# Grouped 1x1 convolution: all pixels in full 128-row chunks on the two hardware DMA queues, with a hardware loop on TensorE

## The chip, the cores and the metric

The kernel runs on one core of one Trainium2 chip. The metric is the device time of one execution in microseconds (us), and lower is better. The kernel before took 528.25 us (median of 3 runs, 526.8 to 528.28). "The span" is the part of the time that the profile covers, from the first to the last instruction.

One look means one profiled run, next to runs of the kernel before on the same chip.

## The reference, cut to what matters

```python
# x: (1, 512, 512, 192) bf16;  w: (1, 1, 4, 48, 48) bf16   (kernel size 1, 4 groups of 48 channels)
xg  = x.reshape(1, 512, 512, 4, 48)
out = einsum('bhwgc,gcd->bhwgd', xg, w[0, 0])      # for each pixel and each group: 48 -> 48
return out.reshape(1, 512, 512, 192)
```

There are 262,144 pixels of 384 bytes. About 100.7 MB are read and 100.7 MB are written, and very little is computed for each byte. In the page of the kernel before, the DMA engines are busy for 90% or more of nearly every slice.

## The kernel before

A chunk is a load of some rows by 32 pixels for each row. A row is one partition of SBUF and 12,288 contiguous bytes of DRAM, and in the trace it is one DMA packet of 12,288 bytes. Normal chunks ("nat") have 128 rows. SyncE issues their loads and ScalarE their stores, both on hardware DMA queues.

Beside them run 24 "relief" chunks of 60 or 44 rows. GpSimd loads and stores them on its software DMA queue. A dummy transfer of one or five rows comes before each. The kernel's helper for it is called `move_cursor`, and I call it the cursor move. The trace shows that in 22 of the 24 relief loads one of the 16 increments lands 11.2 to 16.2 us before the second. I read that as one engine which gets no row of the relief chunk.

```python
NBI = 5; NBO = 5; NRI = 2; NRO = 2; NOB = 5; NXP = 3; NXS = 3; LOOK = 2
RELIEF = {"relA": (36, 60, 1), "relB": (52, 44, 5)}   # first partition, rows, dummy rows
N_RELIEF = 24                                          # 18 relA, 6 relB
...
        @block.gpsimd
            def load(n):
                wait_in_free(wq, n)
                i = ordinal[n] % NRI
                p0_, rows, skip = RELIEF[kinds[n]]
                move_cursor(skip)                      # the dummy transfer
                gp.dma_start(xr_sb[i][p0_:p0_ + rows, 0:sizes[n] * C], rows_view(xf, n)).then_inc(rl_sem[i], 16)
...
        @block.sync
            for n in nat_ids:
                wait_in_free(wq, n)
                b = ordinal[n] % NBI
                sp.dma_start(x_sb[b][:, 0:sizes[n] * C], rows_view(xf, n)).then_inc(ld_sem[b], 16)
...
        @block.tensor                                  # 620 groups, all unrolled
            for g in range(NG):
                if g + LOOK < NG:
                    transposes(g + LOOK)               # 6 transposes of x into PSUM
                matmuls(g)                             # 6 matmuls with block-diagonal weights
```

A group is four pixel columns: 6 transposes, a copy of the transposed pixels from PSUM to SBUF by VectorE, 6 matmuls, and the copy of the outputs by ScalarE and VectorE. A relief chunk costs as many groups as a normal one but has under half of its pixels. That is why there are 620 groups and not 512.

## Time and profile before

| | before |
|---|---|
| time, median of 4 runs beside the kernel after | 527.52 us (525.32 to 528.28) |
| span of the profiled run | 523.9 us |
| TensorE busy | 89% |
| DMA engines busy, middle of the span | 90% or more in nearly every slice |
| bytes moved by DMA | 202.4 MB, mean 386 GB/s |

These lines are from the page of the kernel before: the span, the busy time of the engines, the GB/s in 40 equal slices, the DMA queues (packets, MB, share of the time of 16 engines), the shares of the chain of waits that ended last, and one line of the DMA issues (count, KB each, median us from issue to landing).

```profile
span 523.9 us, 16823 instructions
PE 468.8 (89%) x7450; PEld 462.0 (88%) x7450; DVE 401.5 (77%) x810; ACT 413.8 (79%) x622; POOL 55.3 (11%) x106
...
GB/s 302 295 416 402 392 413 391 397 407 406 386 396 401 417 386 378 415 385 383 419 400 378 419 388 397 415 387 398 417 393 391 414 395 389 415 419 400 376 332 143
...
q1 hardware_dynamic: 8848, 84.17, 41.4%
q10 hardware_dynamic: 8640, 84.15, 39.4%
q0 software_dynamic: 5184, 33.04, 16.1%
q8 instruction: 58, 0.95, 0.7%
...
PE 53%; DMA 45%; POOL 1%; ACT 0%; issue 0%; POOLq 0%; ACTq 0%
...
xr_sb<-in_x_dram POOLq DMA_DIRECT2D x18, 720.0 KB, 19.9
```

The row of GB/s swings between about 378 and 419, although the DMA engines are busy all the time. So the swings are not idle time: some packets take longer. The window view says so directly. Its columns are the stretch in us and its length, then the busy us (and instructions) of five engines, the granted TensorE clock, the DMA share and the GB/s.

```profile
core 0: us, PE busy (x) PEld busy (x) DVE busy (x) ACT busy (x) POOL busy (x), PEclk, DMA share, GB/s
213.00:219.00 6.00, 5.41 (x87) 5.42 (x88) 4.66 (x10) 3.73 (x6) 0.00 (x0) 1.00 1.01 421
222.00:228.00 6.00, 6.00 (x104) 5.99 (x102) 5.33 (x12) 5.33 (x10) 0.23 (x1) 1.00 1.00 341
240.00:246.00 6.00, 6.00 (x109) 5.99 (x106) 5.34 (x13) 5.45 (x10) 0.00 (x0) 1.00 1.00 352
247.00:252.00 5.00, 5.00 (x84) 5.00 (x82) 4.50 (x10) 4.55 (x8) 2.03 (x4) 1.00 1.00 423
```

The DMA share is 1.00 in all four, but the second and third stretch move about a fifth less. These two are relief loads. The first is a relief store, and the fourth has no relief transfer. In the packet records of the whole trace, 24 stretches of this kind last 132 us together. A packet of 12,288 bytes takes 570 ns on average in them and 469 ns outside, and the median of all is 460.0 ns. (The prediction's 23 stretches and 125 us are an earlier count of the same records. The counts depend on where the line is drawn. Counted again, in slices of 2 us whose packets average over 510 ns, there are 25 stretches, 126 us together. This recount is given below where it differs much.)

### The profile page before, as it was taken

What the parts mean: (1) busy time and instruction counts of PE and PEld (TensorE: products, weight loads), DVE (VectorE), ACT (ScalarE), POOL (GpSimd) and SP (SyncE); (2) the same over time, 40 slices, a digit from 0 to 9 for tenths busy, and PEclk for the clock granted to TensorE, in tenths of its full rate; (3) what the DMA queues carried; (4) which work ended last, traced back from release to release, by engine and by line L of the source; (5) the groups of instructions that cost most, each with busy time, mean ns of one, the idle gap of its engine ahead of it and who ended that gap; (6) DMA issues with size and microseconds to landing.
All of it is one profiled execution on the core that took longest, in us unless ns stands there. A gap on an engine that the chain in (4) does not pass through costs nothing.

```text
span 523.9 us, 16823 instructions
## 1 busy us (share of the span) xinstructions
PE 468.8 (89%) x7450; PEld 462.0 (88%) x7450; DVE 401.5 (77%) x810; ACT 413.8 (79%) x622; POOL 55.3 (11%) x106
## 2 busy tenths in 40 slices
PE   6399999999999979879989889879979889997873
PEld 5399999999999979879979889879979879997872
DVE  5188889888888868768878778767878777886751
ACT  6199998989999968768879779778969778895752
POOL 6011011101110110010110110110110110000000
PEclk9699999999999999999999999998999998998987
DMA  8999999999999999999999999999999999999983
GB/s 302 295 416 402 392 413 391 397 407 406 386 396 401 417 386 378 415 385 383 419 400 378 419 388 397 415 387 398 417 393 391 414 395 389 415 419 400 376 332 143
DMA packets 22744, 202.43 MB, mean 386 GB/s; under 512 B 4624, under 2 KB 5648, under 8 KB 6928
## 3 DMA queue, kind: packets, MB, share of 16 engines
q1 hardware_dynamic: 8848, 84.17, 41.4%
q10 hardware_dynamic: 8640, 84.15, 39.4%
q0 software_dynamic: 5184, 33.04, 16.1%
q8 instruction: 58, 0.95, 0.7%
q14 instruction: 14, 0.11, 0.1%
HBM read 100.68 MB, written 100.66 MB: 384 GB/s over the span
## 4 chain that ended last, share of the span: by engine, by line
PE 53%; DMA 45%; POOL 1%; ACT 0%; issue 0%; POOLq 0%; ACTq 0%
DMA x_sb<-in_x_dram 42%; PE o_ps L322 30%; PE xT_ps L300 23%; DMA xr_sb<-in_x_dram 2%; POOL xr_sb L246 1%; ACT o_sb L390 0%; POOL scratch L228 0%; POOL esel L216 0%; POOL esel L212 0%; POOL ident L220 0%; POOL ident L213 0%; POOL scratch L214 0%; ACTq L57 0%; POOLq L415 0%; POOLq L216 0%
## 5 line engine op out<-in xcount | busy, mean ns | idle before, releaser
L354 DVE COPY xT_sb<-xT_ps 128x768 bf16<-128x768 bf16 (+1 forms) x620 | 322.5, 524 | 112.9 <-PE xT_ps L300 109.5
L322 PE MATMUL o_ps<-wt,xT_sb 128*128 128x144 bf16 (+1 forms) x3720 | 367.0, 236 | 0.0
L390 ACT CAST o_sb<-o_ps 128x768 bf16<-128x768 f32 x300 | 231.0, 799 | 76.1 <-PE o_ps L322 74.4
L322 PEld LDWEIGHTS o_ps<-wt,xT_sb 128*128 128x128 bf16 x3720 | 266.2, 99 | 1.4
L300 PE MATMUL xT_ps<-ident,x_sb 128*128 128x128 bf16 x2568 | 219.1, 223 | 39.9 <-DMA x_sb<-in_x_dram 39.7
L300 PEld LDWEIGHTS xT_ps<-ident,x_sb 128*128 128x128 bf16 x2568 | 168.1, 100 | 44.7 <-DMA x_sb<-in_x_dram 43.9
L390 ACT CAST or_sb<-o_ps 128x768 bf16<-128x768 f32 x134 | 101.6, 804 | 10.2 <-PE o_ps L322 7.1
L300 PE MATMUL xT_ps<-ident,xr_sb 96*128 96x96 bf16 x1152 | 81.7, 207 | 8.8 <-DMA xr_sb<-in_x_dram 8.8
L386 ACT CAST o_sb<-o_ps 128x384 bf16<-128x384 f32 x128 | 61.5, 480 | 20.0 <-PE o_ps L322 19.4
L300 PEld LDWEIGHTS xT_ps<-ident,xr_sb 96*128 96x128 bf16 x1152 | 64.6, 98 | 9.0 <-DMA xr_sb<-in_x_dram 9.0
L362 DVE CAST o_sb<-o_ps 128x384 bf16<-128x384 f32 x128 | 70.8, 553 | 1.9 <-PE o_ps L322 1.7
L228 POOL DMA_DIRECT2D scratch<-scratch x48 | 24.2, 504 | 409.3 <-DVE xT_sb L354 409.0
L362 DVE CAST or_sb<-o_ps 128x384 bf16<-128x384 f32 x58 | 32.2, 555 | 0.7
L386 ACT CAST or_sb<-o_ps 128x384 bf16<-128x384 f32 x58 | 28.7, 495 | 0.0
L243 POOL DMA_DIRECT2D out_dram<-or_sb x24 | 12.7, 527 | 0.3 <-issue 0.3
L236 POOL DMA_DIRECT2D xr_sb<-in_x_dram x24 | 12.5, 522 | 0.0
L246 POOL MEMSET xr_sb<- 128x6144 bf16 x1 | 5.2, 5207 | 0.0
L282 PE MATMUL o_ps<-w_sb,esel 48*128 48x48 bf16 x10 | 0.6, 209 | 2.6 <-DMA w_sb<-in_w_dram 2.6
L369 ACT ACTIVATE xr_sb<-xr_sb 128x3072 uint32<-128x3072 uint32 x1 | 2.8, 2763 | 0.0
L282 PEld LDWEIGHTS o_ps<-w_sb,esel 48*128 48x128 bf16 x10 | 0.4, 111 | 2.6 <-POOL esel L216 2.6
L369 ACT ACT_TABLE_LOAD x1 | 1.3, 1283 | 0.8 <-PEq L415 0.8
L339 DVE MEMSET xT_sb<- 128x384 uint32 x3 | 1.1, 378 | 1.0 <-PEq L415 1.0
(10 smaller groups left out, 2.4 us busy)
## 6 DMA issues: line engine op xcount, KB each, us to landing
x_sb<-in_x_dram SPq DMA_DIRECT2D x51, 1536.0 KB, 40.0
out_dram<-o_sb ACTq DMA_DIRECT2D x51, 1536.0 KB, 38.3
xr_sb<-in_x_dram POOLq DMA_DIRECT2D x18, 720.0 KB, 19.9
out_dram<-or_sb POOLq DMA_DIRECT2D x18, 720.0 KB, 12.3
xr_sb<-in_x_dram POOLq DMA_DIRECT2D x6, 528.0 KB, 18.8
out_dram<-or_sb POOLq DMA_DIRECT2D x6, 528.0 KB, 10.9
x_sb<-in_x_dram SPq DMA_DIRECT2D x3, 768.0 KB, 30.0
out_dram<-o_sb ACTq DMA_DIRECT2D x3, 768.0 KB, 11.9
```

The lines of the kernel that those rows point to most:

```text
L228: gp.dma_start(scratch[0:skip, 2 * nd + 1:2 * nd + 2], scratch[0:skip, 0:1]).then_inc(dm_sem, 16)
L236: gp.dma_start(xr_sb[i][p0_:p0_ + rows, 0:sizes[n] * C], rows_view(xf, n)).then_inc(rl_sem[i], 16)
L243: gp.dma_start(rows_view(of, n), or_sb[i][p0_:p0_ + rows, 0:sizes[n] * C]).then_inc(rs_sem[i], 16)
L246: gp.memset(xr_sb[i][:], 0.0).then_inc(z_sem, 1)
L300: last = pe.transpose(xT_ps[:, g % NXP, j * 128:j * 128 + rows], xb[0:rows, col:col + 128], ident[0:rows, 0:rows])
L322: last = pe.matmul(o_ps[:, v % NOB, c0:c1], lhsT=xs[:, j * 128:(j + 1) * 128], rhs=wt[:, WOFF[tc]:WOFF[tc] + (c1 - c0)], start=(tc == 0), ...
L339: dve.memset(xT_sb[i][:], 0.0).then_inc(zt_sem, 1)
L354: dve.tensor_copy(dst, src).then_inc(dve_done, 1)
L362: dve.tensor_copy(obuf(n)[:, u * UC:(u + 1) * UC], o_ps[:, v % NOB, 0:UC]).then_inc(dve_done, 1)
L369: act.memzero(xr_sb[i][:]).then_inc(z_sem, 1)
L386: ins = act.copy(ob[:, u * UC:(u + 1) * UC], o_ps[:, v % NOB, 0:UC])
L390: ins = act.copy(dst, o_ps[:, v % NOB:v % NOB + 2, 0:UC])
```

## The change

The relief chunks and the software queue go. All pixels are in 70 chunks of 128 rows on the two hardware queues, with one more input and output buffer each. TensorE's program, which is all unrolled before, becomes a hardware loop of 10 trips over a body of 48 groups. For this its waits had to stop depending on the group's number: each ring semaphore is waited for at a constant and then counted down by TensorE itself. The intent, as I read it: fewer groups, no software queue, and less fetch of TensorE's program (58 packets on the instruction queue in the page before).

```diff
-NBI = 5
-NBO = 5
-NRI = 2
-NRO = 2
-NOB = 5
-NXP = 3
-NXS = 3
-LOOK = 2
-RELIEF = {"relA": (36, 60, 1), "relB": (52, 44, 5)}
...
-N_RELIEF = 24
...
-ST_DELAY = 1
+NBI = 6
+NBO = 6
+NXP = 4
+NOB = 4
+LOOK = 3
+ST_DELAY = 2
+RING = 6
...
+    body = NBI * PPC // 4
+    loop_g0 = chunk_g0[first_full]
+    reps = max(0, (n_full * PPC // 4 - LOOK) // body)
+    loop_g1 = loop_g0 + reps * body
...
         @block.gpsimd
...
-                gp.dma_start(xr_sb[i][p0_:p0_ + rows, 0:sizes[n] * C], rows_view(xf, n)).then_inc(rl_sem[i], 16)
...
         @block.tensor
...
             def transposes(g):
...
                 if lg == 0:
-                    wait_loaded(wq, n)
+                    pe.wait_ge(ld_sem[n % NBI], 16)
...
+                if lg == 0:
+                    ins[1].then_inc(ld_sem[n % NBI], -16)
...
             def matmuls(g):
...
+                waited = [e1_sem[g % RING]]
+                if g >= 2:
+                    waited.append(fa_sem[(g - 2) % RING])
+                    if shared(g - 2):
+                        waited.append(d2_sem[(g - 2) // 3 % 2])
+                for s in waited:
+                    pe.wait_ge(s, 1)
...
+                for i, s in enumerate(waited):
+                    ins[1 + i].then_inc(s, -1)
...
-            for g in range(NG):
-                if g + LOOK < NG:
-                    transposes(g + LOOK)
-                matmuls(g)
+            for g in range(loop_g0 if reps else 0):
+                step(g)
+            if reps:
+                with pe.Fori(0, reps, 1):
+                    for g in range(loop_g0, loop_g0 + body):
+                        step(g)
+            for g in range(loop_g1 if reps else 0, NG):
+                step(g)
```

More of the change, by code (lines that the diff above doesn't have):

```diff
@@ L27 @@
 TAIL = (16, 8, 4, 4)
-NBI = 5
-NBO = 5
-NRI = 2
-NRO = 2
-NOB = 5
-NXP = 3
-NXS = 3
-LOOK = 2
-RELIEF = {"relA": (36, 60, 1), "relB": (52, 44, 5)}
-REND = 96
-RPPC = 32
-B_EVERY = 4
-N_RELIEF = 24
-FIRST_RELIEF = 4
-RELIEF_GAP = 2
-SHARE = (2, 4, 7)
-ST_DELAY = 1
+NBI = 6
[5 more added lines that the diff above has]
+RING = 6
 class Waiter:
@@ L57, in wait @@
         self.eng.wait_ge(sem, val)
-def relief_kinds(n_relief):
-    return ["relB" if B_EVERY and i % B_EVERY == B_EVERY - 1 else "relA" for i in range(n_relief)]
 def plan_chunks(npix):
     assert npix % 512 == 0, "the pixel count must be a multiple of 512"
-    for n_relief in range(N_RELIEF, -1, -1):
-        rk = relief_kinds(n_relief)
-        rest = npix - sum(RELIEF[k][1] * RPPC for k in rk)
-        if rest < 0 or rest % 512 != 0:
-            continue
-        cols = rest // 128
-        head, tail = list(HEAD), list(TAIL)
-        if cols < sum(head) + sum(tail) + PPC:
-            if n_relief:
-                continue
-            head, tail = [], []
-        mid = cols - sum(head) - sum(tail)
-        nat = head
-        while mid > 0:
-            nat.append(min(PPC, mid))
-            mid -= nat[-1]
-        nat += tail
-        chunks = [("nat", s) for s in nat]
-        pos = FIRST_RELIEF
-        for k in rk:
-            pos = min(pos, len(chunks) - len(tail))
-            chunks.insert(pos, (k, RPPC))
-            pos += RELIEF_GAP + 1
-        return chunks
-    raise AssertionError("no chunk plan")
+    cols = npix // 128
+    head, tail = list(HEAD), list(TAIL)
+    if cols < sum(head) + sum(tail) + PPC:
+        head, tail = [], []
+    mid = cols - sum(head) - sum(tail)
+    first = len(head)
+    full = mid // PPC
+    sizes = head + [PPC] * full
+    if mid % PPC:
+        sizes.append(mid % PPC)
+    return sizes + tail, first, full
 def bass_standalone__grouped__vision_kernel(nc, x, w, out):
@@ L96, in bass_standalone__grouped__vision_kernel @@
     npix = B * H * W_
-    chunks = plan_chunks(npix)
-    n_chunks = len(chunks)
-    kinds = [c[0] for c in chunks]
-    sizes = [c[1] for c in chunks]
-    nrows = [128 if k == "nat" else RELIEF[k][1] for k in kinds]
-    nat_ids = [n for n in range(n_chunks) if kinds[n] == "nat"]
-    rel_ids = [n for n in range(n_chunks) if kinds[n] != "nat"]
-    n_rel = len(rel_ids)
-    ordinal = {n: i for ids in (nat_ids, rel_ids) for i, n in enumerate(ids)}
+    sizes, first_full, n_full = plan_chunks(npix)
+    n_chunks = len(sizes)
     xf = x.rearrange("b h w c -> (b h w) c")
@@ L110, in bass_standalone__grouped__vision_kernel @@
     wv = w.rearrange("a b g c d -> c (a b g) d")
-    chunk_pix0, p0 = [], 0
-    for n in range(n_chunks):
-        chunk_pix0.append(p0)
-        p0 += nrows[n] * sizes[n]
-    assert p0 == npix
-    groups, chunk_g0 = [], []
+    col0, groups, chunk_g0, chunk_g1, c0 = [], [], [], [], 0
     for n, s in enumerate(sizes):
+        col0.append(c0)
+        c0 += s
         chunk_g0.append(len(groups))
         groups += [(n, lg) for lg in range(s // 4)]
+        chunk_g1.append(len(groups))
     NG = len(groups)
-    chunk_g1 = [chunk_g0[n] + sizes[n] // 4 for n in range(n_chunks)]
+    body = NBI * PPC // 4
+    assert body % 12 == 0
+    loop_g0 = chunk_g0[first_full]
+    reps = max(0, (n_full * PPC // 4 - LOOK) // body)
+    loop_g1 = loop_g0 + reps * body
     def shared(g):
-        return (g % 5 == 2) or ((g % 10) in SHARE)
+        return g % 3 == 1 and g < NG - 3
     dve_prog = [("wcopy", 0)]
@@ L133, in bass_standalone__grouped__vision_kernel @@
             dve_prog.append(("ev2", h))
-    dve_cnt = {op: i + 1 for i, op in enumerate(dve_prog)}
-    act_cnt = {g: g + 1 for g in range(NG)}
     def rows_view(ap, n):
-        rows, s = nrows[n], sizes[n]
-        return ap[chunk_pix0[n]:chunk_pix0[n] + rows * s, :].rearrange("(p i) c -> p (i c)", p=rows)
+        s = sizes[n]
+        return ap[128 * col0[n]:128 * (col0[n] + s), :].rearrange("(p i) c -> p (i c)", p=128)
     with ExitStack() as es:
@@ L144, in bass_standalone__grouped__vision_kernel @@
         o_sb = [es.enter_context(nc.sbuf_tensor(f"o_sb{i}", [128, PPC * C], BF16)) for i in range(NBO)]
-        xr_sb = [es.enter_context(nc.sbuf_tensor(f"xr_sb{i}", [128, RPPC * C], BF16)) for i in range(NRI)]
-        or_sb = [es.enter_context(nc.sbuf_tensor(f"or_sb{i}", [128, RPPC * C], BF16)) for i in range(NRO)]
-        xT_sb = [es.enter_context(nc.sbuf_tensor(f"xT_sb{i}", [128, 2 * UC], BF16)) for i in range(NXS)]
+        xT_sb = [es.enter_context(nc.sbuf_tensor(f"xT_sb{i}", [128, 2 * UC], BF16)) for i in range(NXP)]
         ident = es.enter_context(nc.sbuf_tensor("ident", [128, 128], BF16))
@@ L151, in bass_standalone__grouped__vision_kernel @@
         wt = es.enter_context(nc.sbuf_tensor("wt", [128, WCOLS], BF16))
-        scratch = es.enter_context(nc.sbuf_tensor("scratch", [16, 4 * max(n_rel, 1) + 8], BF16))
         xT_ps = es.enter_context(nc.psum_tensor("xT_ps", [128, NXP, 1024], BF16))
@@ L160, in bass_standalone__grouped__vision_kernel @@
         st_sem = [sem(f"st{i}") for i in range(NBO)]
-        rl_sem = [sem(f"rl{i}") for i in range(NRI)]
-        rs_sem = [sem(f"rs{i}") for i in range(NRO)]
-        z_sem = sem("z_sem")
-        zt_sem = sem("zt_sem")
-        w_sem, id_sem, e_sem, wb_sem = sem("w_sem"), sem("id_sem"), sem("e_sem"), sem("wb_sem")
-        p0_sem, p1_sem, sc_sem, dm_sem = sem("p0_sem"), sem("p1_sem"), sem("sc_sem"), sem("dm_sem")
-        t_done = sem("t_done")
-        mm_done = sem("mm_done")
-        dve_done = sem("dve_done")
@@ L170, in bass_standalone__grouped__vision_kernel @@
-        act_done = sem("act_done")
-        def xbuf(n):
-            return x_sb[ordinal[n] % NBI] if kinds[n] == "nat" else xr_sb[ordinal[n] % NRI]
-        def used_rows(n):
-            return 128 if kinds[n] == "nat" else REND
-        def obuf(n):
-            return o_sb[ordinal[n] % NBO] if kinds[n] == "nat" else or_sb[ordinal[n] % NRO]
-        def wait_loaded(wq, n):
-            k = ordinal[n]
-            if kinds[n] == "nat":
-                wq.wait(ld_sem[k % NBI], 16 * (k // NBI + 1))
-            else:
-                wq.wait(rl_sem[k % NRI], 16 * (k // NRI + 1))
@@ L188, in wait_in_free @@
-        def wait_in_free(wq, n):
-            k = ordinal[n]
-            if kinds[n] == "nat":
-                if k >= NBI:
-                    wq.wait(t_done, chunk_g1[nat_ids[k - NBI]])
-            elif k >= NRI:
-                wq.wait(t_done, chunk_g1[rel_ids[k - NRI]])
-        def wait_out_free(wq, n):
-            k = ordinal[n]
-            if kinds[n] == "nat":
-                wq.wait(st_sem[k % NBO], 16 * (k // NBO))
-            else:
-                wq.wait(rs_sem[k % NRO], 16 * (k // NRO))
@@ L203, in wait_evacuated @@
-        def wait_evacuated(wq, n):
-            wq.wait(act_done, act_cnt[chunk_g1[n] - 1])
-            dv = [dve_cnt[("ev2", g)] for g in range(chunk_g0[n], chunk_g1[n]) if shared(g)]
-            if dv:
-                wq.wait(dve_done, max(dv))
+        w_sem, id_sem, e_sem, wb_sem, wc_sem = (sem(s) for s in ("w_sem", "id_sem", "e_sem", "wb_sem", "wc_sem"))
+        p0_sem, p1_sem = sem("p0_sem"), sem("p1_sem")
+        t_done, mm_done = sem("t_done"), sem("mm_done")
+        e1_sem = [sem(f"e1_{i}") for i in range(RING)]
@@ L209, in _ @@
+        fa_sem = [sem(f"fa_{i}") for i in range(RING)]
+        d2_sem = [sem(f"d2_{i}") for i in range(2)]
+        def wait_out_free(wq, n):
+            wq.wait(st_sem[n % NBO], 16 * (n // NBO))
         @block.gpsimd
         def _(gp):
-            wq = Waiter(gp)
             gp.memset(esel[:], 1.0).then_inc(p0_sem, 1)
             gp.memset(ident[:], 1.0).then_inc(p1_sem, 1)
-            gp.memset(scratch[:], 0.0).then_inc(sc_sem, 1)
             gp.wait_ge(p0_sem, 1)
@@ L222, in _ @@
                              channel_multiplier=1).then_inc(id_sem, 1)
-            gp.wait_ge(sc_sem, 1)
-            state = {"nd": 0}
-            def move_cursor(skip):
-                nd = state["nd"]
-                gp.dma_start(scratch[0:skip, 2 * nd + 1:2 * nd + 2], scratch[0:skip, 0:1]).then_inc(dm_sem, 16)
-                state["nd"] = nd + 1
-            def load(n):
-                wait_in_free(wq, n)
-                i = ordinal[n] % NRI
-                p0_, rows, skip = RELIEF[kinds[n]]
-                move_cursor(skip)
-                gp.dma_start(xr_sb[i][p0_:p0_ + rows, 0:sizes[n] * C], rows_view(xf, n)).then_inc(rl_sem[i], 16)
-            def store(n):
-                wait_evacuated(wq, n)
-                i = ordinal[n] % NRO
-                p0_, rows, skip = RELIEF[kinds[n]]
-                move_cursor(skip)
-                gp.dma_start(rows_view(of, n), or_sb[i][p0_:p0_ + rows, 0:sizes[n] * C]).then_inc(rs_sem[i], 16)
-            for i in range(1, NRI if n_rel else 0, 2):
-                gp.memset(xr_sb[i][:], 0.0).then_inc(z_sem, 1)
-            if n_rel:
-                gp.wait_ge(z_sem, NRI)
-            for n in rel_ids[:NRI]:
-                load(n)
-            for k, n in enumerate(rel_ids):
-                store(n)
-                if k + NRI < n_rel:
-                    load(rel_ids[k + NRI])
-            for i in range(NRO):
-                cnt = len(rel_ids[i::NRO])
-                if cnt:
-                    gp.wait_ge(rs_sem[i], 16 * cnt)
-            if state["nd"]:
-                gp.wait_ge(dm_sem, 16 * state["nd"])
         @block.sync
@@ L265, in _ @@
             sp.dma_start(w_sb[:], wv).then_inc(w_sem, 16)
-            for n in nat_ids:
-                wait_in_free(wq, n)
-                b = ordinal[n] % NBI
+            for n in range(n_chunks):
+                if n >= NBI:
+                    wq.wait(t_done, chunk_g1[n - NBI])
+                b = n % NBI
                 sp.dma_start(x_sb[b][:, 0:sizes[n] * C], rows_view(xf, n)).then_inc(ld_sem[b], 16)
@@ L272, in _ @@
         def _(pe):
-            wq = Waiter(pe)
             def build_weights():
-                wq.wait(e_sem, 1)
-                wq.wait(w_sem, 16)
+                pe.wait_ge(e_sem, 1)
+                pe.wait_ge(w_sem, 16)
                 last = None
-                for (tc, r, g, c0) in WBLOCKS:
+                for (tc, r, g, c0_) in WBLOCKS:
                     s0 = ESHIFT - r
-                    col = WOFF[tc] + c0
+                    col = WOFF[tc] + c0_
                     last = pe.matmul(o_ps[:, NOB - 1, col:col + CG], lhsT=esel[:, s0:s0 + 128],
@@ L288, in transposes @@
                 if g == 0:
-                    wq.wait(id_sem, 1)
+                    pe.wait_ge(id_sem, 1)
                 if lg == 0:
-                    wait_loaded(wq, n)
-                xb = xbuf(n)
-                rows = used_rows(n)
-                last = None
+                    pe.wait_ge(ld_sem[n % NBI], 16)
+                xb = x_sb[n % NBI]
+                ins = []
                 for ul in range(2):
@@ L299, in transposes @@
                         j = ul * 3 + tc
-                        last = pe.transpose(xT_ps[:, g % NXP, j * 128:j * 128 + rows],
-                                            xb[0:rows, col:col + 128], ident[0:rows, 0:rows])
-                last.then_inc(t_done, 1)
-            def matmuls(g):
-                xs = xT_sb[g % NXS]
-                last = None
+                        ins.append(pe.transpose(xT_ps[:, g % NXP, j * 128:(j + 1) * 128],
+                                                xb[:, col:col + 128], ident[:]))
@@ new lines, in transposes @@
+                if lg == 0:
+                    ins[1].then_inc(ld_sem[n % NBI], -16)
+                ins[-1].then_inc(t_done, 1)
+            def matmuls(g):
+                xs = xT_sb[g % NXP]
+                waited = [e1_sem[g % RING]]
+                if g == 0:
+                    pe.wait_ge(wc_sem, 1)
+                if g >= 2:
[4 more added lines that the diff above has]
+                    pe.wait_ge(s, 1)
+                ins = []
@@ L307, in matmuls @@
                 for ul in range(2):
                     v = 2 * g + ul
-                    if ul == 0:
-                        need = dve_cnt[("ev1", g)]
-                        if g >= 3:
-                            if shared(g - 3):
-                                need = max(need, dve_cnt[("ev2", g - 3)])
-                            else:
-                                wq.wait(act_done, act_cnt[g - 3])
-                        wq.wait(dve_done, need)
-                    elif g >= 2:
-                        wq.wait(act_done, act_cnt[g - 2])
@@ L319, in matmuls @@
                     for tc in range(3):
                         j = ul * 3 + tc
-                        c0, c1 = COLR[tc]
-                        last = pe.matmul(o_ps[:, v % NOB, c0:c1], lhsT=xs[:, j * 128:(j + 1) * 128],
-                                         rhs=wt[:, WOFF[tc]:WOFF[tc] + (c1 - c0)],
-                                         start=(tc == 0), stop=(tc == 2), skip_group_check=True)
-                last.then_inc(mm_done, 1)
+                        c0_, c1_ = COLR[tc]
+                        ins.append(pe.matmul(o_ps[:, v % NOB, c0_:c1_], lhsT=xs[:, j * 128:(j + 1) * 128],
+                                             rhs=wt[:, WOFF[tc]:WOFF[tc] + (c1_ - c0_)],
+                                             start=(tc == 0), stop=(tc == 2), skip_group_check=True))
@@ L327, in _, with step @@
+                for i, s in enumerate(waited):
+                    ins[1 + i].then_inc(s, -1)
+                ins[-1].then_inc(mm_done, 1)
+            def step(g):
+                if g + LOOK < NG:
+                    transposes(g + LOOK)
+                matmuls(g)
             build_weights()
@@ L337, in _ @@
             wq = Waiter(dve)
-            for i in range(NXS if n_rel else 0):
-                dve.memset(xT_sb[i][:], 0.0).then_inc(zt_sem, 1)
-            if n_rel:
-                dve.wait_ge(zt_sem, NXS)
-            waited_chunk = -1
             for (op, g) in dve_prog:
@@ L345, in _ @@
                     wq.wait(wb_sem, 1)
-                    dve.tensor_copy(wt[:], o_ps[:, NOB - 1, 0:WCOLS]).then_inc(dve_done, 1)
+                    dve.tensor_copy(wt[:], o_ps[:, NOB - 1, 0:WCOLS]).then_inc(wc_sem, 1)
                     continue
@@ L350, in _ @@
                     wq.wait(t_done, g + 1)
-                    rows = used_rows(n)
-                    src = xT_ps[:, g % NXP, 0:2 * UC].rearrange("p (j c) -> p j c", c=128)[:, :, 0:rows]
-                    dst = xT_sb[g % NXS][:].rearrange("p (j c) -> p j c", c=128)[:, :, 0:rows]
-                    dve.tensor_copy(dst, src).then_inc(dve_done, 1)
-                else:
-                    if waited_chunk != n:
-                        waited_chunk = n
-                        wait_out_free(wq, n)
+                    dve.tensor_copy(xT_sb[g % NXP][:], xT_ps[:, g % NXP, 0:2 * UC]).then_inc(e1_sem[g % RING], 1)
+                else:
+                    wait_out_free(wq, n)
                     wq.wait(mm_done, g + 1)
@@ L361, in _ @@
                     v = 2 * g + 1
-                    dve.tensor_copy(obuf(n)[:, u * UC:(u + 1) * UC],
-                                    o_ps[:, v % NOB, 0:UC]).then_inc(dve_done, 1)
+                    dve.tensor_copy(o_sb[n % NBO][:, u * UC:(u + 1) * UC],
+                                    o_ps[:, v % NOB, 0:UC]).then_inc(d2_sem[g // 3 % 2], 1)
         @block.scalar
@@ L367, in _ @@
             wq = Waiter(act)
-            for i in range(0, NRI if n_rel else 0, 2):
-                act.memzero(xr_sb[i][:]).then_inc(z_sem, 1)
             pending = []
             def store(n):
-                wait_evacuated(wq, n)
-                b = ordinal[n] % NBO
+                b = n % NBO
                 act.dma_start(rows_view(of, n), o_sb[b][:, 0:sizes[n] * C]).then_inc(st_sem[b], 16)
@@ L381, in _ @@
                 wq.wait(mm_done, g + 1)
+                while pending and pending[0][1] <= g:
+                    store(pending.pop(0)[0])
                 v = 2 * g
-                ob = obuf(n)
+                ob = o_sb[n % NBO]
                 if shared(g):
@@ L387, in _ @@
                 else:
-                    assert v % NOB != NOB - 1
                     dst = ob[:, lg * 2 * UC:(lg + 1) * 2 * UC].rearrange("p (u c) -> p u c", u=2)
                     ins = act.copy(dst, o_ps[:, v % NOB:v % NOB + 2, 0:UC])
-                ins.then_inc(act_done, 1)
-                if g == chunk_g1[n] - 1 and kinds[n] == "nat":
+                ins.then_inc(fa_sem[g % RING], 1)
+                if g == chunk_g1[n] - 1:
                     pending.append((n, g + ST_DELAY))
-                while pending and pending[0][1] <= g:
-                    store(pending.pop(0)[0])
             for (n, _) in pending:
+                act.wait_ge(fa_sem[(chunk_g1[n] - 1) % RING], 1)
                 store(n)
             for b in range(NBO):
-                cnt = len(nat_ids[b::NBO])
+                cnt = len(range(b, n_chunks, NBO))
                 if cnt:
-                    act.wait_ge(st_sem[b], 16 * cnt)
+                    wq.wait(st_sem[b], 16 * cnt)
 _INS = ['x', 'w']
```

## The prediction

> **What bounds the kernel now.** DMA: the page's slices show the 16 DMA engines 90% busy or more from slice 2 to 38, moving 201.3 MB at 384 GB/s; the chain of waits gives 45% to loads, 53% to TensorE. TensorE (89% busy) is close: relief chunks fill only 60 or 44 of 128 rows, so 620 groups of 0.75 us (timeline) are 465 us; 512 full groups are 384.
>
> In the packet records a 12,288-byte packet takes 460 ns at best, 491 ns on average, and nearly all the excess sits in 23 stretches of 3 to 14 us, together about 125 us, where it averages 574 ns (469 ns outside). These coincide with the relief *loads* on the software queue, not with its stores. The windows view agrees: 222-228 us 341 GB/s, 240-246 us 352; 247-252 us 423, and 213-219 us (a relief store) 421. Outside them the mean is about 417 GB/s.
>
> Bytes by engine, worked out from the relief shapes (60 rows = 15 engines, 44 rows = 11): the engine always left out carries 10.5 MB, most others 12.88 MB: 1,048 packets x 491 ns = 515 us, plus about 10 us of start and end gives the span. One of 16 increments of most transfers lands 15 to 25 us before the next. The relief exists, I infer, because TensorE's instruction fetch (queue table: 58 packets of 16 KB, 0.95 MB, 1.07 us each, 62 us) falls on that engine.
>
> **What the change does.** Removed: the software queue (33 MB) and with it, I expect, the slow stretches; 108 groups of TensorE, VectorE and ScalarE work. Every engine gets 12.58 MB = 1,024 packets: at about 465 ns 476 us; by the observed 417 GB/s, 483 us. Moved: the skipped engine gets 2.1 MB more (about 78 us), affordable only if the loop ends most instruction fetch. [...] If it stays resident, I expect about 10 fetch packets, 11 us, not 58. Added: up to three waits per group and ten trips of the loop; TensorE's slack (384 of 480 us) should hide them.
>
> **Sum.** 476 to 483 us of DMA + 11 us fetch on one engine + 2 us start + 5 us end = 494 us span, +4 us between span and measured time = 498 us. The DMA saving is on the critical path; the freed compute is not.
>
> **If the loop refetches its body each trip**, one engine carries 12.58 MB plus about 50 us of fetch: about 540 us. I give that 20 to 25%, hence 488 to 538. Chances: faster 0.75, same 0.12, slower 0.13.
>
> **What would show it right:** no slow stretches, mean 12 KB packet under 470 ns; 405-420 GB/s over the middle of the span; instruction queue 58 packets to 15 or fewer; TensorE waiting for loads; the 16 landings of a load within a few us. **Wrong:** instruction packets near 50 and one engine landing far behind the rest (fetch not removed); packets still at 490 ns (relief loads not the cause); TensorE idle once per 48 groups (branching); or groups over 0.94 us with loads landed (waits, four output banks).

What is cut here is the argument about the size of the loop's body, which no trace or run showed. No term of the sum is cut: it came to 494 us of span and 498 us of time. Its 11 us of fetch are 10 packets at the 1.07 us that a fetch packet took in the trace before. The 10 was my estimate. (58 packets for 620 groups are 7.5 for the 80 groups that TensorE's program now holds: the 48 of the body and the 32 outside the loop.) That all fetch falls on one engine was an inference. The bytes by engine, with 15 engines for 60 rows and 11 for 44, are an estimate from the shapes of the chunks. Later traces show four rows for each of 16 engines in loads of 64 rows and 15 engines for 60 rows; for 44 rows nothing shows it.

## The result, and the profile after

The kernel after takes 494.0 us (median of 4 runs, 493.32 to 495.58), against 527.52 us before. The ratio is 0.9379, with a 95% interval from 0.935 to 0.9409, so the change is faster. A ratio here is the mean time of one kernel's runs over that of the other's of the same rounds, so it is not quite the ratio of the medians that are quoted.

The lines of the page after that answer to those of before:

```profile
span 492.4 us, 14343 instructions
PE 415.0 (84%) x6154; PEld 389.1 (79%) x6154; DVE 358.1 (73%) x683; ACT 345.6 (70%) x513; POOL 1.3 (0%) x8
...
GB/s 294 414 418 425 427 427 429 430 429 429 430 429 429 429 428 427 427 429 427 428 430 429 429 430 430 429 430 427 428 427 429 428 429 429 429 429 427 279 253 143
...
q1 hardware_dynamic: 10288, 100.69, 48.5%
q10 hardware_dynamic: 10080, 100.67, 48.3%
q8 instruction: 7, 0.11, 0.1%
...
DMA 71%; PE 24%; ACT 3%; issue 1%; ACTq 1%; SPq 0%
```

Two of the same stretches in the window view after, with the columns as before:

```profile
222.00:228.00 6.00, 4.80 (x75) 4.49 (x73) 4.33 (x10) 4.08 (x7) 0.00 (x0) 1.00 1.02 432
240.00:246.00 6.00, 4.84 (x75) 4.50 (x72) 4.17 (x8) 4.33 (x8) 0.00 (x0) 1.00 1.01 430
```

The largest wait of TensorE in the view of waits (who waited for what: us in total, times, longest us):

```profile
PE xT_ps L184 <- DMA x_sb<-in_x_dram: 58.3, 54, 3.2
```

The last load in the chain of waits (start, duration, what), with the transposes that it releases:

```profile
453.46 28.42 DMA x_sb<-in_x_dram
481.93 0.82 PE xT_ps L184 x6
```

The bytes are the same (HBM read and written together differ by less than 0.1%), and the DMA engines are as busy as before. They move them faster: 425 to 430 GB/s through the middle, against a swing from 378 to 419. The mean packet of 12,288 bytes went from 492.5 to 462.3 ns. TensorE now waits for loads 54 times. The chain of waits moved from 53% TensorE to 71% DMA. The queue of instruction fetch went from 58 packets to 7.

So far everything looks as predicted, the total included (498 predicted, 494 measured). The experiments ask whether the reasons were right.

### The profile page after: what moved, and what is told of

Read it like the earlier page. It is cut to its first block, busy times and chain, and to the rows that moved or that the text cites. A ratio compares the mean times of both kernels' runs of the same rounds, so it can differ in the third digit from the quotient of the medians.

```text
span 492.4 us, 14343 instructions
## 1 busy us (share of the span) xinstructions
PE 415.0 (84%) x6154; PEld 389.1 (79%) x6154; DVE 358.1 (73%) x683; ACT 345.6 (70%) x513; POOL 1.3 (0%) x8
## 4 chain that ended last, share of the span: by engine, by line
DMA 71%; PE 24%; ACT 3%; issue 1%; ACTq 1%; SPq 0%
DMA x_sb<-in_x_dram 71%; PE o_ps L207 13%; PE xT_ps L184 10%; ACT o_sb L274 3%; ACTq L258 1%; SPq L155 0%; SPq L150 0%; ACTq L47 0%
## 5 line engine op out<-in xcount | busy, mean ns | idle before, releaser
L242 DVE COPY xT_sb<-xT_ps 128x768 bf16<-128x768 bf16 x512 | 283.8, 555 | 114.8 <-PE xT_ps L184 109.7
L274 ACT CAST o_sb<-o_ps 128x768 bf16<-128x768 f32 x342 | 267.0, 799 | 107.9 <-PE o_ps L207 101.6
L184 PE MATMUL xT_ps<-ident,x_sb 128*128 128x128 bf16 x3072 | 257.2, 220 | 58.3 <-DMA x_sb<-in_x_dram 58.3
L207 PE MATMUL o_ps<-wt,xT_sb 128*128 128x144 bf16 (+1 forms) x3072 | 297.4, 233 | 10.4 <-ACT o_sb L274 10.1
L184 PEld LDWEIGHTS xT_ps<-ident,x_sb 128*128 128x128 bf16 x3072 | 195.0, 98 | 70.0 <-DMA x_sb<-in_x_dram 68.9
L207 PEld LDWEIGHTS o_ps<-wt,xT_sb 128*128 128x128 bf16 x3072 | 211.5, 98 | 24.5 <-issue 17.7
L271 ACT CAST o_sb<-o_ps 128x384 bf16<-128x384 f32 x170 | 81.6, 480 | 33.3 <-PE o_ps L207 24.0
L248 DVE CAST o_sb<-o_ps 128x384 bf16<-128x384 f32 x170 | 94.2, 554 | 8.1 <-PE o_ps L207 7.0
```

The source lines that it names most:

```text
L184: ins.append(pe.transpose(xT_ps[:, g % NXP, j * 128:(j + 1) * 128], xb[:, col:col + 128], ident[:]))
L207: ins.append(pe.matmul(o_ps[:, v % NOB, c0_:c1_], lhsT=xs[:, j * 128:(j + 1) * 128], rhs=wt[:, WOFF[tc]:WOFF[tc] + (c1_ - c0_)], start=(tc ...
L242: dve.tensor_copy(xT_sb[g % NXP][:], xT_ps[:, g % NXP, 0:2 * UC]).then_inc(e1_sem[g % RING], 1)
L248: dve.tensor_copy(o_sb[n % NBO][:, u * UC:(u + 1) * UC], o_ps[:, v % NOB, 0:UC]).then_inc(d2_sem[g // 3 % 2], 1)
L271: ins = act.copy(ob[:, u * UC:(u + 1) * UC], o_ps[:, v % NOB, 0:UC])
L274: ins = act.copy(dst, o_ps[:, v % NOB:v % NOB + 2, 0:UC])
```

## The experiments

The expectations use letters, and a letter stands for what the text says beside it. In short: A is my theory as it then stood. In the first batch it is the prediction's: that TensorE's instruction fetch falls on the engine which the relief left out, so that the relief can only go if the loop comes. In the second batch it is that the software queue's loads stretch the packets, and, for the run on the slow engine, that taking work from that engine shortens the time. B is the first rival: the fetch does not matter, and the relief costs more than it gives, with or without the loop. C and D are the rivals in the second batch: C puts the stretch on the shape and placement of the relief loads, whichever queue issues them, and D says that software loads of full rows are harmless. E is the rival for the run on the slow engine: the engine is the wrong one, or software stores stretch packets as well. F is C made exact: the place of a partial load decides, so that 64 rows stretch the packets from partition 36 and not from partition 32.

The texts say "engine 4" for the engine that had 11 labels in the second experiment. The number is only a name: no trace gives an engine's number.

"Slow stretches" are counted in the packet records as in the section on the profile before. All kernels below gave the correct result.

### Take the relief out, and nothing else

```diff
-N_RELIEF = 24
+N_RELIEF = 0
```

This is the kernel before, still unrolled, with its own buffers and waits.

> The kernel before with the relief chunks taken out (all chunks 128 rows, two hardware queues, TensorE still unrolled). Theory A (fetch falls on one engine, slow stretches come from the relief loads): mean 12 KB packet falls from 491 to under 470 ns, no slow stretches, about 48 fetch packets (58 x 512/620) of 1.07 us all on one engine, which ends about 51 us or more after the others would; time 535 to 555 us, slower than before (528). Rival B (the fetch does no harm, the software queue was pure loss): time 494 to 502 us, no engine far behind. Rival C (the slow stretches are not due to relief loads): mean packet stays near 490 ns, time about 550 us or more.

Measured: 493.99 us (4 runs, 492.95 to 494.04), ratio 0.9351 (0.9322 to 0.9379). Theory A failed, and B held. From the page of this run:

```profile
span 492.1 us, 13861 instructions
...
GB/s 283 422 426 426 425 427 427 425 427 426 428 428 427 429 426 426 428 426 425 425 427 429 428 426 428 428 427 428 424 426 425 426 428 427 429 428 425 362 305 137
...
q8 instruction: 48, 0.79, 0.6%
```

There are 48 fetch packets, and yet the row of GB/s is as flat as after the whole change. There is no slow stretch, and the mean packet takes 463.0 ns. One edited number gives all of the gain that the large diff gives.

### Tell the engines apart, in the kernel after

The trace does not name the engine of a DMA packet. This run adds 15 tiny loads, of 1 to 15 rows, on the load queue, after chunk 30:

```diff
                 sp.dma_start(x_sb[b][:, 0:sizes[n] * C], rows_view(xf, n)).then_inc(ld_sem[b], 16)
+                if n == 30:
+                    for r in range(1, 16):
+                        m = 1 if r == 1 else 32 * r
+                        sp.dma_start(lab[0:r, 512 * r:512 * r + m], rows_view(xf, 30)[0:r, 0:m]).then_inc(lab_sem, 16)
+            sp.wait_ge(lab_sem, 16 * 15)
```

> The kernel after, plus 15 tiny loads (r rows, r = 1 to 15, each of its own size) issued once on the load queue, so that in the packet records every DMA engine can be named by how many of them it served [...]. Time: within 1% of the kernel after (494 us). Theory A (some engine is slow for a reason of its own): the lagging chain of packets, 478 ns per 12 KB packet against 460 ns on the others, is one named engine, and it is not one that fetched instructions during the loop. Rival B (the lag is leftover instruction fetch): the lagging chain is the one that has the 16 KB or 8 KB instruction packets.

Measured: 494.18 us (one run), so the labels cost nothing that this run shows. I chained the packets into 16 back-to-back sequences, which I take for the 16 engines, and the sequences had 0, 1, 2, ... 15 labels, each count once. So an engine can be told by its number of labels.

The sequence that lagged had 11 labels. I call it the slow engine. Its packets of 12,288 bytes took 478.4 ns on average, while 13 engines without other traffic took 460.0 ns. In the stretch looked at (150 to 320 us) the slow engine had no fetch packet at all, and TensorE's own fetch packets (16,384 bytes) all lay before 53 us or after 468 us. So it is slow for some other reason.

### Unroll TensorE again, in the kernel after

```diff
-    reps = max(0, (n_full * PPC // 4 - LOOK) // body)
+    reps = 0
```

The labels are in this run and the next too.

> The kernel after with TensorE's loop taken out (same instructions, unrolled), and the same 15 tiny label loads. Theory A: about 48 to 52 fetch packets instead of 7, all on one named engine, whose transfers end late; the other 15 engines wait for it; time 535 to 555 us, within 1.5% of the kernel before without relief. Rival B (the loop matters little, all of the gain is the removal of relief): 494 to 502 us.

Measured: 497.39 us (4 runs, 496.19 to 498.28), ratio 0.9414 (0.9385 to 0.9443). Theory A failed, and B held. The instruction queue in the page of this run:

```profile
q8 instruction: 50, 0.82, 0.6%
```

The fetch is back, but it is spread over eight of the 16 sequences (about 6 packets each). A fetch packet takes 966 ns on average, so each of the eight gives about 6 us to it (50 packets of 0.966 us over eight). The trace shows a little more: behind 48 of the 50 the next data packet took 887 ns on average and not 460, so each engine gives nearer 9 us (an estimate). The slow engine, the one with 11 labels, has none. It is still the slowest, with 480.4 ns per packet. Beside it the other engines have some 18 us to spare (an estimate: 1,024 packets, 478 ns against 460), so fetch on them can cost little.

The loop is worth 3.4 us here (494.0 against 497.4, from two batches, and the two sets of runs do not overlap), which is 0.7%. It only wins back what the new structure costs: the old unrolled structure without relief ran at 493.99 us on the same chip as this run. Which part of the new structure costs it is open.

### A loop body of twice the length

```diff
-    body = NBI * PPC // 4
+    body = 2 * NBI * PPC // 4
```

That is 96 groups and 5 trips.

> The kernel after with a loop body of 96 groups in 5 trips instead of 48 in 10 [...], and the label loads. Theory A (what counts is that the body stays resident): the fetch comes back, about 45 to 55 packets, time 530 to 555 us as unrolled. Rival B (a loop as such saves the fetch, or the whole body is held at this size too): 7 to 15 packets and 494 us.

Measured: 497.64 us (4 runs, 497.37 to 498.15), ratio 0.943 (0.9402 to 0.9457). The instruction queue, from the page, and one line of the view of waits:

```profile
q8 instruction: 56, 0.92, 0.7%
...
PE xT_ps L191 <- issue: 24.2, 5, 6.3
```

The body of 48 groups runs ten times with 7 fetch packets in the whole kernel. The body of 96 has 56, more than the 50 of the unrolled program, which I read as a body that is fetched anew on its trips. It also stalls TensorE four times, once for each jump back between the five trips, by 5.6 to 6.3 us (the fifth wait in that line is one of 0.2 us, at 73.7 us). So the part of theory A about the fetch held, and its consequence for the time did not: refetching everything costs 3.6 us against the kernel after, and not the 40 us and more of my second case. TensorE has slack for the stalls: its waits for loads fell from 58.3 to 30.8 us. The engines that carry the fetch have it for the packets (the 18 us of the estimate above).

### Put relief-like loads back: three variants

The first of these runs adds 24 loads to the kernel after. They copy 60 rows that are also loaded anyway to partitions 36 to 95 of an unused buffer, on the software queue, each after a cursor move. The second issues the same loads on the hardware load queue. The third goes back to the software queue, with the same number of bytes as 128 rows of 5,760 bytes. All read the same extra 17.7 MB, so all are slower than the kernel after, and the question is by how much.

```diff
+            for i, n in enumerate(EXTRA):          # 24 of the chunks
+                ...
+                gp.dma_start(scratch[0:1, 2 * i + 1:2 * i + 2], scratch[0:1, 0:1]).then_inc(dm_sem, 16)
+                gp.dma_start(xr_sb[i % 2][36:96, :], rows_view(xf, n)[0:60, :]).then_inc(rl_sem[i % 2], 16)   # first
+                sp.dma_start(xr_sb[i % 2][36:96, :], rows_view(xf, n)[0:60, :]).then_inc(rl_sem[i % 2], 16)   # second
+                gp.dma_start(xr_sb[i % 2][:, 0:15 * C], rows_view(xf, n)[:, 0:15 * C]).then_inc(rl_sem[i % 2], 16)  # third
```

(The three `dma_start` of the extra loads belong to one run each. The dummy transfer is in the first run only.)

> The kernel after plus 24 extra loads of 60 rows x 12,288 B on the software queue, placed and cursor-moved as the relief loads were, whose data nobody uses, and the 15 label loads. Bytes alone: 15 engines get 96 packets more, 44 us at 460 ns, so about 538 us. Theory A (relief loads on the software queue stretch everybody's packets): 24 slow stretches of 4 to 7 us in which hardware-queue packets average over 540 ns, mean 12 KB packet 475 ns or more, time 555 to 570 us. Rival B (the stretches came from how relief chunks were computed on, or from the mix of whole kernel before): packets stay at 460 to 465 ns, 535 to 545 us.

> The same 24 extra loads of 60 rows, same bytes and destinations, issued on the hardware load queue in place of the software queue. Theory A (the software queue is what stretches): packets at 460 to 466 ns, 535 to 545 us. Rival C (any extra load of 60 rows into these partitions stretches the others): as the run with software loads, mean packet 475 ns or more.

> The same 17.7 MB on the software queue, but as 24 loads of all 128 rows x 5,760 B (all 16 engines, no cursor moves). Theory A (software loads as such): slow stretches again, hardware packets over 540 ns inside them, 550 us or more. Rival D (the 60-row shape[...] is what stretches): packets stay at 460 to 466 ns, about 535 to 540 us.

Measured, one look each:

| extra loads | time (us) | mean packet (ns) | slow stretches |
|---|---|---|---|
| software, 60 rows at partition 36 | 563.48 | 484.2 | 22, 125 us |
| hardware, 60 rows at partition 36 | 572.74 | 491.0 | about 102 us |
| software, 128 rows | 537.6 | 462.3 | 2, 4 us |

The rows of GB/s from the three pages, in this order:

```profile
GB/s 236 329 378 395 414 408 403 426 413 400 428 413 403 428 409 421 419 401 415 397 396 398 425 394 408 415 408 405 421 403 405 415 402 423 424 425 419 309 205 185
```

```profile
GB/s 312 371 399 425 428 426 430 428 405 341 427 414 378 419 404 407 404 390 355 410 418 346 407 418 340 388 427 377 397 423 409 391 391 406 371 400 343 162 284 295
```

```profile
GB/s 297 427 423 428 428 426 427 431 427 428 428 429 429 427 430 427 424 432 427 427 433 424 432 427 430 431 424 433 425 428 427 430 432 424 427 434 410 237 219 241
```

In the recount of stretches these are 22 and 104 us, 25 and 106 us, and 2 and 4 us, so the first two differ little.

A time alone would have kept my theory alive: the first run fell into its range of 555 to 570 us. The second run takes the software queue away, and the swing stays and goes deeper. The third keeps the software queue, and the swing is gone. So the queue is not the cause. The shape or the place of the loads is.

### Place alone: the same 64 rows, four partitions further

These are hardware loads again, and now only the first partition differs.

```diff
-                    sp.dma_start(xr_sb[i % 2][32:96, :], rows_view(xf, n)[32:96, :]).then_inc(rl_sem[i % 2], 16)
+                    sp.dma_start(xr_sb[i % 2][36:100, :], rows_view(xf, n)[32:96, :]).then_inc(rl_sem[i % 2], 16)
```

In a load of 64 rows each of 16 engines gets four rows (the trace of the run at partition 32 shows four packets for each). The trace shows no partition numbers of packets, so the pair can show that the place matters, but not why. The 60 hardware rows at partitions 36 to 95 stretched too (572.74 us).

> The kernel after plus 24 extra loads of 64 rows x 12,288 B on the hardware load queue into partitions 32 to 95. All 16 engines take 4 rows each (96 packets more per engine, 44 us): about 540 us if nothing is stretched. Theory F [...]: packets stay at 460 to 466 ns, 535 to 545 us. Rival G (any extra load of part of the partitions stretches): mean packet 475 ns or more, 555 us or more, like the 60-row runs.

> The same loads, same source rows, same queue, same 16 engines, but into partitions 36 to 99, four further on. Theory F: [...] slow stretches appear, mean packet 475 ns or more, 555 to 575 us. Rival G: same as the run into 32 to 95, whichever that is. Rival H (only transfers on fewer than 16 engines stretch): packets at 460 to 466 ns, 535 to 545 us, in both.

Measured: 537.73 us at partition 32, 576.34 us at partition 36, one look each on the same chip. The lines from the two pages, partition 32 first:

```profile
GB/s 316 412 421 425 427 429 431 427 430 430 426 431 427 429 429 427 422 426 431 429 427 430 429 428 426 433 428 426 432 427 427 431 429 428 429 431 365 294 264 245
...
q1 hardware_dynamic: 12448, 119.64, 53.0%
```

```profile
GB/s 317 354 396 414 430 428 422 426 391 422 425 344 354 419 377 387 418 334 423 418 407 418 417 404 344 411 417 330 367 419 352 386 426 334 416 394 408 226 275 301
...
q1 hardware_dynamic: 12448, 119.64, 55.3%
```

The queue, packets, bytes and source rows are equal. At partition 36 there are 25 slow stretches, 109 us together, with a mean packet of 678 ns in them, and the whole run is 38.6 us longer. At partition 32 there are two, of 5 us together. In the recount these are 27 and 120 us, and 4 and 8 us. Theory F held in both.

### Software loads without the cursor move

This is the first of the three variants above without its dummy transfers.

```diff
-                gp.dma_start(scratch[0:1, 2 * i + 1:2 * i + 2], scratch[0:1, 0:1]).then_inc(dm_sem, 16)
```

> The run with 24 software loads of 60 rows again, without the one-row moves of the cursor[...]. Theory F: [...] at least one of the 24 loads whose own and neighbouring packets stay under 470 ns and others over 560. Rival G/H: all loads stretch alike (550 ns, within what the run with fixed cursor showed), time about 560 us.

Measured: 565.02 us (one look). Every one of the 24 loads stretched the packets of the others, to between about 520 and 630 ns (means over the time of each load). F expected at least one load under 470 ns, and there was none. F took for granted that without the cursor moves each load would leave out another engine than the load before it, so that one of them would happen to fit. The trace shows that it did not. Around the load at 236.7 us the engines can be told by their labels: the 15 that have 1 to 15 labels take rows of it, and the one without a label takes none. And in every full load from 76 to 440 us the first of the 16 increments lands 9.6 to 31.5 us before the second, so one engine is left out again and again. If the loads took turns, each engine would be left out once or twice, which is under 4 us (an estimate: four packets of 460 ns each time), and with the 64-row loads, which leave out none, the lead is at most 1.1 us.

So this run did not vary what F needed, and the failure of its expectation does not speak against F. All its loads are at partition 36, and all stretch, as the 60 rows there on the hardware queue do.

### The kernel before with its relief, on hardware queues at partition 32

```diff
-RELIEF = {"relA": (36, 60, 1), "relB": (52, 44, 5)}
+RELIEF = {"relA": (32, 60, 1), "relB": (32, 44, 5)}
...
-            for n in rel_ids[:NRI]:
-                load(n)
...
-            for n in nat_ids:
+            for n in range(n_chunks):
                 wait_in_free(wq, n)
+                if kinds[n] != "nat":
+                    ...
+                    sp.dma_start(xr_sb[i][p0_:p0_ + rows, 0:sizes[n] * C], rows_view(xf, n)).then_inc(rl_sem[i], 16)
```

(ScalarE stores the relief chunks in the same way.) All 620 groups and the uneven bytes stay. The queue and the place of the relief change, and the dummy transfers go with the software queue.

> The kernel before with its 24 relief chunks kept (60 and 44 rows, TensorE unrolled, 620 groups), but loaded and stored by the two hardware queues and placed from partition 32 instead of 36 and 52[...]. The uneven bytes stay[...]. Theory F (of the 33 us that relief costs, about two thirds are stretched packets, caused by the misplaced loads, the rest the 24 extra packets on the busy engines, 11.5 us at the 479 ns of engine 4): no slow stretches, mean packet under 470 ns, time 503 to 515 us, between the kernel before (527) and the one without relief (494). Rival J (the loss is the uneven bytes and the 108 extra groups, stretched packets are hidden): 522 us or more. Rival K (relief costs nothing but its stretched packets): 498 us or less.

Measured: 510.19 us (4 runs, 509.21 to 510.98) against 527.03 us of the kernel before on the same chip, ratio 0.9684 (0.9637 to 0.9731). Two lines from its page:

```profile
GB/s 249 415 413 425 427 426 421 422 419 422 422 422 422 420 419 422 419 420 420 422 418 421 420 421 418 421 418 420 424 414 396 417 410 419 401 379 381 326 248 139
...
q8 instruction: 58, 0.95, 0.7%
```

Theory F held in its range of 503 to 515 us. Two slow stretches of 8 us are left of 24 and 132 us (6 and 16 us of 25 and 126 us in the recount). This splits what the relief cost: of about 33 us, 16.8 us (527.03 to 510.19) go with the queue and the place of the relief, and 16.2 us (510.19 to 493.99) with the relief itself. An estimate of the second part: by the shapes of the chunks, at four rows for each engine, the heaviest engines carry 1,048 packets and not 1,024, and 24 packets of 479 ns are 11.5 us; the mean packet is 469.3 ns and not 463.0, which over 1,048 packets is 6.6 us more. The sum, 18 us, is near 16.2. F had put about two thirds of the cost on the place of the loads, and the runs show half. The 108 extra groups of computation come and go with the relief in every run, so their share of the second part is not shown. The first part changes queue and place at once. That the place is enough by itself is shown by the pair before, and not by this run.

### Spare the slow engine

In the kernel after, the last of the 16 increments of a load falls further and further behind the fifteenth, to 12.0 us in the load that lands from 448.7 us on, and I take it for the slow engine's. In this run five stores are split: rows 0 to 119 go out on the software queue after a cursor move that was meant to leave the slow engine without a row, and rows 120 to 127 on the hardware queue. (That the move does this was my assumption, and the 35 packets less that the text gives to this engine are an estimate that rests on it.)

```diff
+            for i, n in enumerate(SPLIT):          # chunks 16, 26, 36, 46, 56
+                gp.wait_ge(mm_done, chunk_g1[n] + ST_DELAY)
+                skip = 5 if i == 0 else 1
+                gp.dma_start(scratch[0:skip, 2 * i + 1:2 * i + 2], scratch[0:skip, 0:1]).then_inc(dm_sem, 16)
+                gp.dma_start(rows_view(of, n)[0:120, :], o_sb[n % NBO][0:120, :]).then_inc(sw_sem[n], 16)
...
-                act.dma_start(rows_view(of, n), o_sb[b][:, 0:sizes[n] * C]).then_inc(st_sem[b], 16)
+                r0 = 120 if n in SPLIT else 0
+                act.dma_start(rows_view(of, n)[r0:128, :], o_sb[b][r0:128, 0:sizes[n] * C]).then_inc(st_sem[b], 16)
```

> The kernel after, with five of its 70 stores split: rows 0 to 119 on the software queue [...], rows 120 to 127 on the hardware queue. Engine 4, named by the labels as the one at 478 ns per packet, has 35 packets less (17 us), the others 2 or 3 more. Theory A (engine 4's pace alone sets the end, and software stores do no harm): span 478 to 484 us, time 480 to 486, all 16 engines ending within about 4 us; faster than after by 1.6 to 2.8%. Rival E (the slow engine is not the one named, or software stores stretch packets too): 494 us or slower.

Measured: 499.65 us (6 runs, 498.62 to 500.85), ratio 0.9485 (0.9461 to 0.951). That is slower than the kernel after by 5.6 us. The packets of the split stores took 580 ns on average, and the row of GB/s has a dip for each:

```profile
GB/s 284 418 427 425 426 430 428 429 428 386 414 428 429 431 429 356 415 428 429 428 431 413 390 422 433 429 426 423 399 416 407 427 427 431 386 410 417 312 278 264
```

Theory A's number failed, and E's held. But the edit did not do what was meant, so theory A was not tested. This run has no labels, but one back-to-back sequence stands out by packets of 476 to 479 ns before each of the first four stores, as the slow engine does in the labelled runs (485 ns from 225 to 237 us in the run with software loads behind a cursor move, on the same chip). It carries rows of all four of these stores; in the first two, which can be followed cleanly, the sequence that carries none is one of 460.0 ns. (The fifth store can't be read in this way.) So the slow engine was not spared, and whether sparing it helps stays open. What in these stores slows the packets is not shown: no run of stores takes place, shape and queue apart. The relief stores of the kernel before, of 60 rows, ran at 421 GB/s without a dip, so a rule for stores is not settled.

No run beat the kernel after by more than the spread. The one-number change to the kernel before ties with it.

## Why the prediction was right or wrong

- **Relief loads stretch the packets, and the stretches vanish: right.** 24 stretches and 132 us before, one of 3 us after, and the mean packet 462.3 ns ("under 470" was the mark). The middle of the span is better than my 405 to 420 GB/s: 425 to 430.
- **"Removed: the software queue (33 MB) and with it, I expect, the slow stretches": right in effect, wrong in its reading.** It is not the queue. The same loads on a hardware queue stretch as much (572.74 us), and full-row software loads do not (537.6 us). The place in SBUF is enough: 64 rows at partition 36 cost 38.6 us more than at partition 32.
- **"TensorE's instruction fetch ... falls on that engine": wrong. This is the step that failed.** The fetch goes to eight engines, about 6 to 9 us each when all is unrolled, and to none of them long enough to matter.
- **"Affordable only if the loop ends most instruction fetch" and "about 540 us" without it: wrong with it.** Without the relief and with 48 fetch packets the kernel before takes 493.99 us, and the kernel after, unrolled, 497.39 us. The loop is worth 3.4 us. The 20 to 25% that I gave to 540 us rested on this, and so did the wide upper end of the range.
- **The body of 48 groups stays resident: right, as far as the fetch shows.** 7 packets, 56 with a body of 96, where each jump back stalls TensorE by up to 6.3 us.
- **The sum of 494 us of span: right, but from a wrong term.** I summed 476 to 483 us of DMA, 11 us of fetch on one engine, and a few more. Measured span: 492.4 us. There is no engine with 11 us of fetch: the 7 fetch packets took 996 ns on average, 7 us on all engines together. The 4 us that I put between span and time are 1.9 (494.27 and 492.4 in the profiled run). In the place of the fetch stands the slow engine (478.4 and 480.4 ns in the two runs above, and 477.9 ns in the labelled run at partition 32, on another chip): 1,024 packets of 478 ns are 490 us, while 1,024 of 460 ns are 471 us. The two terms happen to be of like size, so the right sum is luck here.
- **"The 16 landings of a load within a few us": wrong.** In one load near the middle of the kernel after, fifteen increments landed from 231.1 to 236.2 us and the last at 242.6 us. I take that for the slow engine again.
- **TensorE waits for loads, and the freed compute is not on the critical path: right.** TensorE waits 58.3 us for loads in 54 waits. The kernel before with its 620 groups, but with its relief on the hardware queues at partition 32, still waits 37.6 us for loads. No run takes out the groups alone.

Why the slow engine is slow stays open. It carries no fetch of TensorE in the traces where engines could be told apart, and it is slow with the loop and without. All of this is in profiled runs.

## What to carry to other kernels

A DMA engine that is busy all the time can still be slowed: compare bytes per second, and not only the busy share, stretch by stretch (1.00 in both, and 341 against 421 GB/s, in the kernel before), and try a partial load at another place (here 64 rows from partition 32 took 537.73 us and from 36 took 576.34 us). A hand-made balance of the load deserves the cheapest test there is, which is to set it to zero, before a large rewrite is credited with a gain that this one number gives. And a total that comes out right does not prove its terms: undo each part alone.
